# Batch 0 by halves of heads, paired columns and smaller edits at both ends of a fused attention and feed-forward kernel

## The chip, the core and the metric

The kernel runs on one core of a Trainium2 chip. A core has five engines with queues of their own: TensorE (PE in the profile, with its weight loads as PEld), VectorE (DVE), ScalarE (ACT), GpSimd (POOL) and SyncE (SP), which here only issues DMAs. The metric is device time in microseconds for one execution, the median of several runs.

## What is computed

A linear attention (softmax of q over the features of a head, softmax of k over the sequence) feeds a feed-forward layer with a gated activation:

```python
q_s = softmax(q, axis=-1);  k_s = softmax(k, axis=2)          # 8 batches, 8 heads, 576 rows, 64 features
kv  = einsum('bhsd,bhse->bhde', k_s, v)
x   = einsum('bhsd,bhde->bhse', q_s, kv)                      # reshaped to 4608 x 512
h   = x @ w_in                                                # 512 x 2048
g   = h * sigmoid(beta * h)
out = g @ w_out                                               # 2048 x 512, float32
```

Inputs and output are float32; products run in bfloat16 with float32 sums. The sigmoid is made from tanh: g = (tanh(beta h / 2) + 1) h, with a factor two taken out of the attention part.

## The kernel before

**Tiling.** The 4608 rows are nine chunks of 512: the first 512 rows of each of the eight batches, in a layout where a partition holds nine consecutive sequence rows, and one chunk (number 7) that gathers the last 64 rows of all batches. The hidden dimension of 2048 is 16 units of 128. Unit n of the 144 (chunk n // 16, block n % 16) has a first product `h_n` (`st1`, line 867: four matmuls of 512 columns, 128 contraction rows each, weights from `w_in_b`), a tanh on ScalarE (`th_n`, line 899), a gate on VectorE (`g_n`, line 909), and a second product `o_n` (`st2`, line 937: four matmuls, into four PSUM banks `acc` that collect over the 16 units of a chunk). The other four PSUM banks, `ring`, are dealt out in turn (`take`, line 206) to first products, transposes, x blocks and the small products of the attention part.

**Attention per batch.** q: maximum over features (VectorE, line 378), subtraction (GpSimd, 393), exponential (ScalarE, 422), sum (VectorE, 428), reciprocal (433), multiplication (GpSimd, 441), then a transpose: by TensorE for batches 0 and 1 (464), by a DMA from SP for the others (448), which waits until the tail product (`xt`, 734) of the batch two before has read the buffer. k: a maximum by partitions with a 32 by 32 transpose (490), its reduction (`kred`, 501), an exchange between halves of 64 partitions (batch 0: a float32 matmul with a permutation, `kswap`, 507; others: four small reductions, 522), the maximum spread out again (`krep`, 550), subtraction (GpSimd, 560), exponential (612). Then `kv` (638), its scaling (`kvn`, 657 to 660), x (688) and its cast into SBUF (`xev`).

**Batch 0** goes in thirds of the rows (rows 0 to 3, 4 to 7 and 8 of a partition's nine). k of heads 0 to 3 (`KPE`) is subtracted on TensorE: an identity matmul puts k into PSUM (580), a second one with a negative identity adds minus the maximum (593), and the exponential reads PSUM (600, 605). x of batch 0 is made for one half of the rows at a time, all heads; so the first four units (`LEAD`) run by halves of rows: 256 columns, tanh of two units per bank and a gate over two units.

**Weights.** w_in and w_out come in eight blocks w0 to w7 (even: four units of w_in, odd: four units of w_out), each in two DMAs of 512 KB into four buffers `wst`, and are cast to bfloat16 on GpSimd or ScalarE (line 320). A unit's w_in columns are 128 neighbours; its w_out rows too, 2 KB for each.

**Order.** The whole program is one list, `ORDER` (line 17), of named operations, with the engine of some. An engine runs its operations in the order in which they stand there; a DMA stands on SP in the same way. Semaphores hold an operation until its inputs are there, and whatever stands behind it on the same engine waits with it. `fill` operations are matmuls on zeros (or on q's exponentials) whose results nobody reads; they stand before the first unit only.

**End.** In the last chunk the output block t = 3 is made in two halves of 256 columns; the second half sits in a ring bank and is copied in two pieces of 128, each with its own store (`LAST_PIECES`, line 928).

Of the kernel before, what the change touches and what calls it, by code (L numbers as in the profile page):

```python
# [13 lines left out]
EPS = 1e-9  # L14
# [15 lines left out]
qnorm_0_2_1=pool, xev_0_0_1=act, x_0_1_0, fill_10, fill_5, cast_w2_0=pool, ld_w2_1, xev_0_1_0=dve, ld_w1_0, ld_w1_1,  # L30
cast_w2_1=pool, h_0_0_0, h_0_0_1, h_1_0_0, h_1_0_1, h_0_1_0, xev_0_1_1=act, th_0_0, th_1_0, h_0_1_1, qmax_1_2,
h_1_1_0, h_1_1_1, ld_w4_0, g_0_0, ld_w4_1, qmax_1_3, h_2_0_0, h_2_1_0, ld_k1_0, th_0_1, th_1_1, g_0_1, qsub_1_1=pool,
ld_k1_1, h_2_0_1, h_3_0_0, h_3_0_1, th_3_0, th_2_0, g_2_0, h_2_1_1, h_3_1_0, h_3_1_1, th_2_1, h_6, th_3_1, g_2_1,
h_4, qexp_1_1, qsum_1_1, th_4, g_4, h_5, qexp_1_0, th_5, qsum_1_0, h_7, cast_w1_0=pool, ld_w3_0, o_0_1,
cast_w1_1=pool, o_1_1, o_0_0, o_1_0, qexp_1_2, g_5, qtrt_0, o_2_0, qsum_1_2, qrcp_1_0, th_6, th_7, qexp_1_3, g_6,
ld_w6_0, ld_w6_1, o_3_0, o_2_1, o_3_1, cast_w4_0=pool, qnorm_1_0=pool, qtrtev_0_0=act, ld_w3_1, qtrtev_0_1=dve,
qsum_1_3, g_7, qrcp_1_1, qnorm_1_1=pool, cast_w4_1=act, h_8, th_8, cast_w3_0=pool, kmax_1_0, kmax_1_1, g_8,
cast_w6_0=pool, kmax_1_3, kmax_1_2, kred_1, ksmall_1, krep_1, ld_w5_0, qtr_1_0, qtrev_1_0=act, h_10, th_10, h_9,
qtr_1_1, th_9, h_11, g_10, qtrev_1_1=act, o_4, o_5, th_11, ld_w5_1, cast_w6_1=act, ksub_1_0=pool, cast_w3_1=act,
ld_v1_0, ld_v1_1, ld_w7_0, h_14, kexp_1_1, g_11, h_12, h_15, th_14, ld_q2_1, g_9, cast_w5_0=pool, th_12, g_14, g_12,  # L40
h_13, th_13, kexp_1_0, th_15, ksub_1_1=pool, g_15, ld_q2_0, o_6, o_7, o_8, o_9, vcast_1_0=pool, ld_k2_1, g_13,
# [1028 lines left out]
```

## Time and profile before

| | |
|---|---|
| median of 3 runs | 287.04 us (286.77 to 288.16) |
| profiled execution, its own time | 287.31 us |
| its span, first to last instruction | 285.5 us |
| TensorE busy | 275.8 us, 97% |
| VectorE, ScalarE, GpSimd busy | 194.9, 174.2, 131.2 us |
| DMA | 50.01 MB, mean 175 GB/s |
| granted TensorE clock | 0.999 |

The page of the profile has the busy time of each engine, the span in 40 slices of 7.1 us (a digit is a tenth busy), the DMA queues, the chain of work that ended last, and groups of instructions as `line engine operation out<-in shapes xcount | busy us, mean ns of one | idle before, releaser`. In the chain a row is `start us, duration us, what`. In a row by stretches stand the stretch, its length, each engine's busy time with its count (PE, PEld, DVE, ACT, POOL), the granted clock, the share of the DMA engines and GB/s. A row of the timeline is `start us, duration us, engine line operation, count, [idle before, releaser]`; neighbours that overlap are merged in it. A DMA issue has KB and the median time from issue to landing.

### The profile page before, as it was taken

How to read it: one execution, taken by the hardware profiler on the slowest of the kernel's cores; microseconds unless marked ns; L12 is line 12 of the kernel's file. 1: busy time of each engine (PE TensorE's matmuls, PEld its weight loads, DVE VectorE, ACT ScalarE, POOL GpSimd, SP SyncE). 2: the span in 40 equal slices, each digit the busy share in tenths (PEclk: the TensorE clock that was granted, in tenths of full speed). 3: DMA queues.
4: the chain of work that ended last, by engine and by line, in shares of the span. 5: the costliest groups of instructions: out<-in, count | busy, mean ns of one | idle time of the engine just before them, and what ended most of it. 6: DMA issues, size and time to landing. Idle time of an engine off the chain costs nothing.

```text
span 285.5 us, 5163 instructions
## 1 busy us (share of the span) xinstructions
PE 275.8 (97%) x1947; PEld 129.9 (45%) x1977; DVE 194.9 (68%) x394; ACT 174.2 (61%) x291; POOL 131.2 (46%) x93
## 2 busy tenths in 40 slices
PE   7799999999999999999999999999999999999994
PEld 2356544444444544444444544444444444444442
DVE  2998957999899898997667858555754263435421
ACT  2498885887488577837586566564671274345422
POOL 6899996869379948083960650090020000000000
PEclk9999999999999999999999999999999999999999
DMA  7999999990991994991434927000054001005104
GB/s 229 390 391 385 384 389 391 390 336 7 276 371 43 316 275 181 295 329 41 152 119 113 189 62 193 0 3 2 0 141 164 0 0 39 0 0 187 73 0 147
DMA packets 37048, 50.01 MB, mean 175 GB/s; under 512 B 15760, under 2 KB 16160, under 8 KB 37024
## 3 DMA queue, kind: packets, MB, share of 16 engines
q1 hardware_dynamic: 36880, 49.63, 53.4%
q8 instruction: 15, 0.25, 0.3%
q10 hardware_dynamic: 144, 0.07, 0.1%
q14 instruction: 9, 0.07, 0.1%
HBM read 36.71 MB, written 9.44 MB: 162 GB/s over the span
## 4 chain that ended last, share of the span: by engine, by line
PE 91%; DMA 4%; ACT 1%; SPq 1%; issue 1%; DVE 0%
PE hT L889 43%; PE acc L959 42%; DMA kf<-in_k_dram 2%; DMA wst<-in_moe_w_in_dram 2%; PE hT L638 2%; PE hT L688 1%; SPq L275 1%; PE hT L951 1%; PE acc L951 1%; ACT w_in_b L232 0%; PE hT L464 0%; PE hT L734 0%; ACT qT L232 0%; ACT ek L612 0%; ACT ek L605 0%
## 5 line engine op out<-in xcount | busy, mean ns | idle before, releaser
L907 ACT ACTIVATE th<-hT,beta_c 128x512 bf16<-128x512 f32 (+1 forms) x148 | 96.6, 677 | 66.9 <-PE hT L889 48.5
L924 DVE SCALAR_TENSOR_TENSOR g<-th,hT 128x512 bf16<-128x512 bf16 x144 | 94.6, 680 | 58.5 <-ACT th L907 55.5
L959 PE MATMUL acc<-w_out_b,g 128*128 128x512 bf16 x543 | 130.7, 379 | 1.4 <-issue 0.8
L889 PE MATMUL hT<-xT,w_in_b 128*128 128x512 bf16 (+1 forms) x517 | 117.7, 372 | 0.7 <-issue 0.2
L889 PEld LDWEIGHTS <-w_in_b 128*128 128x128 bf16 x592 | 57.6, 98 | 64.8 <-ACT w_in_b L232 0.2
L959 PEld LDWEIGHTS <-g 128*128 128x128 bf16 x560 | 53.7, 98 | 64.5 <-issue 2.9
L560 POOL TENSOR_TENSOR kf<-kf,kmb 128x1152 f32<-128x1152 f32 (+1 forms) x15 | 38.0, 2543 | 23.6 <-DVE kmb L550 17.6
L441 POOL TENSOR_TENSOR qn<-eqe,qz 128x1152 bf16<-128x1152 bf16 (+2 forms) x20 | 34.5, 1739 | 28.0 <-DVE qz L433 18.1
L393 POOL TENSOR_TENSOR qf<-qf,qm 128x1152 f32<-128x1152 f32 (+2 forms) x20 | 34.4, 1733 | 18.4 <-issue 11.9
L378 DVE TENSOR_REDUCE qm<-qf 128x9 f32<-128x576 f32 (+2 forms) x34 | 23.3, 704 | 6.2 <-DMA qf<-in_q_dram 6.2
L422 ACT ACTIVATE eqe<-qf 128x576 bf16<-128x576 f32 (+2 forms) x34 | 21.5, 657 | 9.5 <-POOL qf L393 9.5
L232 ACT CAST xT<-hT 128x512 bf16<-128x512 f32 x19 | 12.6, 740 | 21.1 <-PE hT L688 21.1
L428 DVE TENSOR_REDUCE qs<-eqe 128x9 f32<-128x585 bf16 (+2 forms) x34 | 24.0, 713 | 0.5 <-ACT eqe L422 0.4
L490 DVE TRANSPOSE_TENSOR_REDUCE km<-kf 128x18 f32<-128x576 f32 x32 | 23.6, 754 | 0.0
L612 ACT ACTIVATE ek<-kf 128x576 bf16<-128x576 f32 x30 | 19.5, 683 | 0.9 <-DMA vf<-in_v_dram 0.9
L234 POOL CAST va<-vf 128x1152 bf16<-128x1152 f32 (+1 forms) x11 | 12.0, 1105 | 6.9 <-DMA vf<-in_v_dram 6.9
L889 PE MATMUL hT<-xTt,w_in_b 128*128 128x512 bf16 x63 | 14.9, 379 | 0.1
L234 DVE CAST xT<-hT 128x512 bf16<-128x512 f32 x9 | 6.3, 728 | 7.0 <-PE hT L688 7.0
L232 ACT COPY osb<-acc 128x512 f32<-128x512 f32 x14 | 7.8, 594 | 3.0 <-PE acc L959 3.0
L367 PE MATMUL hT<-g,warm 128*128 128x512 bf16 x21 | 7.0, 482 | 1.6 <-POOL g L240 1.5
L234 DVE COPY osb<-acc 128x512 f32<-128x512 f32 (+1 forms) x6 | 3.8, 632 | 4.9 <-PE acc L951 3.8
L638 PEld LDWEIGHTS <-ek 64*64 64x64 bf16 x576 | 5.7, 106 | 2.2 <-issue 1.3
(74 smaller groups left out, 121.7 us busy)
## 6 DMA issues: line engine op xcount, KB each, us to landing
qf<-in_q_dram SPq DMA_DIRECT2D x14, 576.0 KB, 6.9
kf<-in_k_dram SPq DMA_DIRECT2D x14, 576.0 KB, 7.7
vf<-in_v_dram SPq DMA_DIRECT2D x14, 576.0 KB, 8.4
out_dram<-osb SPq DMA_DIRECT2D x19, 256.0 KB, 2.6
wst<-in_moe_w_in_dram SPq DMA_DIRECT2D x8, 512.0 KB, 7.9
wst<-in_moe_w_out_dram SPq DMA_DIRECT2D x8, 512.0 KB, 11.2
out_dram<-wst SPq DMA_DIRECT2D x16, 256.0 KB, 3.7
qf<-in_q_dram SPq DMA_DIRECT2D x4, 288.0 KB, 4.1
```

Of the source, the lines that this page charges most:

```text
L234: eng.tensor_copy(dst, src)
L378: dve.tensor_reduce(qm[:, j : j + n, i0:i1], qf[b % 2][:, j : j + n, i0:i1], axis=AX.X, op=ALU.max,)
L393: eng.tensor_tensor(x, x, m, ALU.subtract)
L422: act.activation(eq[:, i0:i1, j : j + n, :].rearrange("p i j d -> p j i d"), x, ACTF.Exp)
L428: dve.tensor_reduce(qs[:, i0:i1, j : j + n].unsqueeze(3), x, axis=AX.X, op=ALU.add)
L441: eng.tensor_tensor(qn[b % 2][:, i0:i1, j : j + n, :], eq[:, i0:i1, j : j + n, :], z, ALU.mult)
L490: dve.tensor_reduce(km[:, j : j + n].rearrange("p j i e -> p (j i e)"), kf[b % 2][:, j : j + n].rearrange("p j i (e c) -> p (j i e) c", c=32),
L560: eng.tensor_tensor(x, x, m, ALU.subtract)
L889: pe.matmul(w, w_in_b[:, kt, u * P : (u + 1) * P], r, start=(kt == 0), stop=(kt == KT - 1),)
L907: act.activation(th[turn(n, h) % 3][:, c], bank(n, h), ACTF.Tanh, scale=beta_c[:, u : u + 1])
L924: dve.scalar_tensor_tensor(out=out, in0=of, scalar=1.0, in1=src, op0=ALU.add, op1=ALU.mult)
L959: pe.matmul(acc[t][:], g[n % NG][:, t * P : (t + 1) * P], w_out_b[:, u, :], start=(u == 0), stop=(u == NJ - 1),)
```

## The change

1. **Batch 0 by halves of heads.** `kred`, `kswap`, `ksmall`, `kvn` and x of batch 0 are done for heads 0 to 3 (J = 0) and 4 to 7 (J = 1) apart. x is made for all 512 rows of one half of the features. The TensorE path for k (`KPE`, `k_in`, `k_minus`, `minus`) is gone; k pieces 0 and 2 are subtracted on VectorE, 1 and 3 on GpSimd.
2. **q of batch 0 by bias.** For rows 0 to 3 and 4 to 7 of heads 0 to 3 the maximum is negated and given to the exponential as a bias, one instruction of 64 columns per row and pair of heads (sixteen in all), with no subtraction.
3. **First units by halves of features.** Units 0 to 3 run all 512 columns, with contraction blocks 0 and 1 (heads 0 to 3) apart from 2 and 3. Units 2 and 3 use banks of `acc`. Tanh and gate are those of every other unit.
4. **Batch 1's k by halves**, in the manner of batch 0: two `kswap` matmuls in place of the small reductions, four subtractions of one piece (two on VectorE through PSUM) in place of two of two pieces on GpSimd.
5. **Columns dealt in pairs.** Unit u takes every second column of a 256-column block of w_in (the even or the odd ones) and the w_out rows that match. A partition of w_out then gets two neighbouring rows, 4 KB at a time, and the weight load reads `w_in_b` with a step of two. Each 256-column block in `w_in_b` is followed by 64 unused columns. beta is transposed with the same step.
6. **Last rows in 384 and 128.** Output block t = 3 of the last chunk in two pieces, 384 columns in `acc` and 128 in a ring bank, one copy and one store each.
7. **A new `ORDER`** throughout, with a new order of loads.

```diff
+consts, ld_q0_1, ld_q0_0, qmax_0_0_j1, qmax_0_0_j0, qmax_0_1_j1, qmax_0_2_0, qexp_0_0_j1, ld_q0_3, qexp_0_0_j0,
+ld_q0_2, qsub_0_2_0=pool, qmax_0_1_j0, qsum_0_0_0, qrcp_0_0_0, qexp_0_2_0, qexp_0_1_j1, qexp_0_1_j0, ld_k0_1,
+qmax_0_1_1, qsub_0_1_1=pool, qmax_0_0_1, qsub_0_0_1=pool, ld_beta, ld_k0_0, ld_v0_0, ld_k0_3, ld_v0_1, kmax_0_1,
+kmax_0_0, qsum_0_1_0, ld_k0_2, ld_v0_2, fill_0, fill_5, fill_7, fill_10, fill_14, ld_v0_3, ld_w0_0, kred_0_0,
+qrcp_0_1_0, qexp_0_1_1, fill_12, fill_6, fill_1, qnorm_0_0_0=pool, fill_3, fill_13, fill_4, kswap_0_0, qtr_0_0_0,
+kmax_0_3, ksmall_0_0, krep_0_1, qexp_0_0_1, qsum_0_0_1, qnorm_0_1_0=pool, ld_w0_1, fill_8, qtrev_0_0_0=act, kmax_0_2,
+qtr_0_1_0, vcast_0_j0=act, fill_2, ksub_0_1=pool, qtrev_0_1_0=act, qrcp_0_0_1, krep_0_0, ld_w2_0, ld_w2_1, kred_0_1,
+ld_q1_1, vcast_0_j1=act, kswap_0_1, qnorm_0_0_1=pool, ksub_0_0=dve, kexp_0_1, ksmall_0_1, fill_11, beta_tr, krep_0_3,
+krep_0_2, kexp_0_0, qtr_0_0_1, ksub_0_3=pool, vcast_0_j3=act, cast_w0_0_1=act, qsum_0_1_1, ksub_0_2=dve, kexp_0_2,
+qrcp_0_1_1, kv_0_0, kexp_0_3, kvn_0_0, ld_w1_0, qmax_0_2_1, qtrev_0_0_1=dve, fill_9, x_0_0, xev_0_0=dve,
+vcast_0_j2=pool, kv_0_1, qnorm_0_1_1=pool, cast_w0_1_0=pool, kvn_0_1, qsub_0_2_1=pool, cast_w0_0_0=pool, qtr_0_1_1,
+xev_0_1=act, h_2_0, h_3_0, cast_w2_0=pool, qtrev_0_1_1=act, ld_w1_1, cast_w2_1=pool, x_0_1, xev_0_3=dve, ld_w4_0,
+cast_w0_1_1=act, qexp_0_2_1, qsum_0_2_0, qsum_0_2_1, qrcp_0_2, qnorm_0_2_1=pool, cast_w1_0=pool, h_0_0, h_1_0,
+ld_w4_1, xev_0_2=act, beta_ev, h_1_1, th_1, ld_q1_0, ld_w3_0, h_0_1, qmax_1_2, h_3_1, h_2_1, ld_k1_1, ld_w6_0,
+qmax_1_3, th_0, g_0, th_2, h_5, g_2, th_5, g_1, th_3, ld_w6_1, g_3, qsub_1_1=pool, h_6, h_4, h_7, th_4, g_5, th_6,
+g_4, g_6, ld_w3_1, cast_w1_1=pool, o_0, o_1, o_2, o_3, qnorm_0_2_0=pool, cast_w4_0=pool, qexp_1_2, qexp_1_3,
+qsum_1_3, qsum_1_2, qrcp_1_1, th_7, ld_k1_0, ld_w5_0, qnorm_1_1=pool, ld_w5_1, g_7, cast_w3_0=pool, ld_v1_0,
...
+st_2_2, xt_3, qnorm_6_0=pool, qexp_7_0, qexp_7_1, xtev_3_0=act, kv_5_0, xtev_3_1=dve,
...
+o_142_0, o_137_3_0, o_141_2, o_143_0, o_142_2, o_143_2, o_138_1, o_139_1, oev_8_0=dve, st_7_2, st_8_0, o_138_3_0,
+o_140_1, o_141_1, o_142_1, o_143_1, o_139_3_0, o_140_3_0, oev_8_1=act, o_141_3_0, o_142_3_0, o_143_3_0,
+oev_8_3_0=act, oev_8_2=dve, st_8_2, o_136_3_1, o_137_3_1, o_138_3_1, o_139_3_1, o_140_3_1, o_141_3_1, st_8_1,
+st_8_3_0, o_142_3_1, o_143_3_1, oev_8_3_1=dve, st_8_3_1
...
-    KPE = range(2)
-    QPE = set()
+    BIAS = {(0, 0), (1, 0)}
...
-    w_in_b = sbt("w_in_b", [P, KT, FF], BF16)
+    w_in_b = sbt("w_in_b", [P, KT, NJ // 2, 2 * P + 64], BF16)
...
-    w_out_v = w_out.rearrange("(j p) f -> p j f", p=P)
+    w_out_v = w_out.rearrange("(m p r) f -> p m r f", p=P, r=2)
...
-                for c, (c0, c1) in enumerate(((0, P), (P, 512))):
+                for c, (c0, c1) in enumerate(((0, 2 * P), (2 * P, 512))):
...
+    def q_exp_rows(j, n, i0, i1):
...
+        for a in range(j, j + n):
+            for i in range(i0, i1):
+                act.activation(eq[:, i, a, :], qf[0][:, a, i, :], ACTF.Exp, bias=qm[:, a, i : i + 1])
...
+    def k_swap(b, J):
...
         pe.matmul(
-            place[("swap", b)][:, 0 : 2 * KT],
+            place[("swap", b, J)][:, 0:4],
             swap[:],
-            kmr[:, :, :, 0].rearrange("p j e -> p (j e)"),
+            kmr[:, k_cut(J), :, 0].rearrange("p j e -> p (j e)"),
...
+            for b in range(2):
+                to = pool if j % 2 else dve
+                op(f"krep {b} {j}", lambda b=b, j=j, to=to: k_rep(b, j, 1, to))
+                op(f"ksub {b} {j}", lambda e, b=b, j=j: k_sub(b, j, 1, e), "pool" if j % 2 else "dve")
...
+    def x_mm(b, J):
...
+            for jp in range(2):
+                place[("x", b, 2 * J + jp)] = acc[2 * jp + J][:]
...
+    SPARE = {2: 0, 3: 2}
...
             pe.matmul(
                 w,
-                w_in_b[:, kt, u * P : (u + 1) * P],
-                r,
+                w_in_b[:, kt, u // 2, u % 2 : 2 * P : 2],
+                x[:, kt],
...
-    LAST_PIECES = ((0, 0, 256), (1, 0, 128), (1, 128, 128))
+    PIECES = ((0, 384), (384, 512))
```

More of the change, by code (lines that the diff above doesn't have):

```diff
@@ L382, in q_max @@
             op=ALU.max,
+            negate=minus,
         )
@@ L928 @@
[L928 to L937 removed]
+        v = NJ // 2 * (u % 2) + u // 2
+        uses("st1", n)
+        if n >= 3:
+            uses("gate", n - 3)
+        made("tanh", n)
+        act.activation(th[n % 3][:], place[("h", n)], ACTF.Tanh, scale=beta_c[:, v : v + 1])
```

569 lines of the change are left out of this document (210 added, 359 removed).

## The prediction, made before the changed kernel was run

> **What bounds the kernel now.** I read the page first: the span, the busy shares, and the row of TensorE beside the row of the DMA engines.
>
> ```profile
> span 285.5 us, 5163 instructions
> PE 275.8 (97%) x1947; PEld 129.9 (45%) x1977; DVE 194.9 (68%) x394; ACT 174.2 (61%) x291; POOL 131.2 (46%) x93
> ...
> PE   7799999999999999999999999999999999999994
> ...
> DMA  7999999990991994991434927000054001005104
> ```
>
> The DMA engines are full for eight slices (57 us), yet from the third slice TensorE is full too. So I looked at when the real work begins and what TensorE idles after that: the chain of waits in order of time, then the busy time of each engine by stretches.
>
> ```profile
> 4.03 6.47 DMA kf<-in_k_dram
> ...
> 20.67 7.01 PE hT L889 x48
> ...
> 40.78 4.32 PE acc L959 x20
> ```
>
> ```profile
> 20.67:60.00 39.33, 39.01 (x282) 19.80 (x284) 32.63 (x68) 32.53 (x56) 31.77 (x25) 1.00 1.05 388
> ...
> sum 261.33, PE 259.05 PEld 122.02 DVE 180.65 ACT 162.50 POOL 114.85; mean PE 51.81 PEld 24.40 DVE 36.13 ACT 32.50 POOL 22.97
> ```
>
> The first unit starts at 20.67 us. From there to 282 us TensorE is busy 259.05 of 261.33 us, and one 512-column matmul takes 4.32/20 = 0.216 us. The kernel is thus three terms: a prelude of 20.67 us, in which batch 0 has to come through; some 261 us of TensorE work, which the change does not shorten (the same 1152 matmuls, 248.8 us at 0.216); and a tail. A gain can come from an earlier start and the tail; a loss from TensorE waiting again, or from dearer matmuls.
>
> **When data lands.** One q or k piece of batch 0 is 288 KB. The rows are DMA issues with the time to landing (the first q piece, then the second half of the first weight block), that weight's issue on SP, the first maximum that needs the fourth q piece, and the rate.
>
> ```profile
> qf<-in_q_dram SPq DMA_DIRECT2D x1, 288.0 KB, 2.9
> ...
> wst<-in_moe_w_in_dram SPq DMA_DIRECT2D x1, 512.0 KB, 7.2
> ```
>
> ```profile
> 9.80 1.09 SPq L316 DMA_DIRECT2D wst<-in_moe_w_in_dram  x2
> ...
> 7.63 1.48 DVE L378 TENSOR_REDUCE qm<-qf 128x8 f32<-128x512 f32 x3 [1.68 <-DMA qf<-in_q_dram]
> ...
> 14.00:16.00 2.00, 1.85 (x11) 1.15 (x10) 1.93 (x7) 1.95 (x5) 1.95 (x2) 1.00 1.05 390
> ```
>
> The fourth piece (1.18 MB) lands at about 7.6, the eighth (the chain) at 10.5, and the last of w0, 5.18 MB in all, at about 10.5 + 7.2 = 17.7. All lie near 4.5 + MB/0.39. In the new order q1's first half (0.59 MB) goes behind the weights, so w0's halves land at 14.9 and 16.2 instead of 16.4 and 17.7. The new order of k and v gives k pieces at 8.3, 9.0, 10.5, 12.0 and the last v at 13.5.
>
> **The new prelude, by its queues.** Durations, from the groups kept apart by shape:
>
> ```profile
> L490 DVE TRANSPOSE_TENSOR_REDUCE km<-kf 128x18 f32<-128x576 f32 x32 | 23.6, 754 | 0.0
> L612 ACT ACTIVATE ek<-kf 128x576 bf16<-128x576 f32 x30 | 19.5, 683 | 0.9 <-DMA vf<-in_v_dram 0.9
> L441 POOL TENSOR_TENSOR qn<-eqe,qz 128x512 bf16<-128x512 bf16 x4 | 4.1, 1046 | 0.3
> L393 POOL TENSOR_TENSOR qf<-qf,qm 128x512 f32<-128x512 f32 x4 | 4.1, 1046 | 2.1 <-DVE qm L378 2.1
> L378 DVE TENSOR_REDUCE qm<-qf 128x8 f32<-128x512 f32 x4 | 2.6, 681 | 1.7 <-DMA qf<-in_q_dram 1.7
> L428 DVE TENSOR_REDUCE qs<-eqe 128x8 f32<-128x520 bf16 x4 | 2.6, 674 | 0.0
> L234 DVE CAST xT<-acc 128x512 bf16<-128x512 f32 x2 | 1.4, 740 | 0.2 <-ACT beta_c L349 0.2
> L560 POOL TENSOR_TENSOR kf<-kf,kmb 128x576 f32<-128x576 f32 x1 | 1.4, 1411 | 0.1
> L560 DVE TENSOR_TENSOR kf<-kf,hT 128x576 f32<-128x576 f32 x1 | 0.7, 715 | 0.0
> L378 DVE TENSOR_REDUCE qm<-qf 128x2 f32<-128x128 f32 x2 | 0.6, 284 | 4.5 <-DMA qf<-in_q_dram 4.5
> L422 ACT ACTIVATE eqe<-qf 128x128 bf16<-128x128 f32 x2 | 0.5, 302 | 1.7 <-POOL qf L393 1.7
> L501 DVE TENSOR_REDUCE kmr<-km 128x8 f32<-128x72 f32 x8 | 1.8, 224 | 0.1
> L550 DVE STREAM_TRANSPOSE hT<-kmx 128x64 f32<-128x64 f32 x1 | 0.3, 260 | 0.0
> L530 DVE TENSOR_TENSOR kmx<-kmr,hT 128x8 f32<-128x8 f32 x1 | 0.2, 151 | 0.0
> ```
>
> VectorE is the tightest queue. From the fourth q piece at 7.6 it runs, without a gap, two maxima of q, four of k, three sums, two subtractions of k (now one piece each), and eleven small operations (four spreads at 0.26, the rest 0.15 to 0.22): 1.36 + 3.02 + 2.02 + 1.43 + 2.29 = 10.1 us by means. Neighbours overlap by about 0.07 (a 1.48 us row for what are 0.68 + 0.68 + 0.28 by means), 22 of them 1.5 us, so it ends near 16.2. GpSimd runs beside it (two q subtractions, four q divisions, two k subtractions, one v cast, the fourth division ending near 18.0). ScalarE ends the last exponential of k at about 17.7.
>
> Heads 0 to 3 are through first: their k-by-v product is done at about 15.9, its scaling on VectorE 16.1 to 17.0, their two x blocks are in SBUF at 18.5 (0.74 each, one on VectorE, one on ScalarE). Units 2 and 3 then run two of their four matmuls each, 0.86 us from 18.6. The second half's scaling ends at 19.1, its x product at 19.7, its casts at 20.6. Meanwhile units 0 and 1 run two matmuls each (weights cast at 19.6). From 20.7 TensorE has all it needs, with 8 matmuls (1.73 us) behind it: as good as a start at 18.97. **Term 1: 18.97 − 20.67 = −1.7 us**, bounds −2.3 and −0.9 (one k exponential sooner; or 0.1 us more at each of eight hand-overs between engines).
>
> The sixteen exponentials with a bias replace two 512-wide ones and two GpSimd subtractions. No row shows 64 columns; the 128-wide row gives 0.30 as an upper bound. Sixteen at that are 4.8 us, begun at 4.2 (the first q piece lands at 0.7 + 2.9, its maximum takes under 0.68) and over by 9.0 at worst, ahead of the sum that needs them (10.2). Cover: the wait for k. They cost nothing; the identity-matmul path removed for k (L580, L593) freed TensorE only where it was waiting.
>
> **Batch 1's k by halves.** Two more small matmuls land in the full stretch, in float32 with four columns. Batch 0 has one; its two passes, its two loads and the matmul behind it:
>
> ```profile
> 13.42 0.39 PE L507 MATMUL hT<-kmr,swap 128*128 128x8 f32 x2
> 13.66 0.59 PE L367 MATMUL hT<-eqe,warm 128*128 128x512 bf16 x2
> ```
>
> ```profile
> 13.42 0.30 PEld L507 LDWEIGHTS hT<-kmr,swap 128*128 128x128 f32 x2
> ```
>
> It holds TensorE for 13.66 − 13.42 = 0.24 us; bounds 0 and 0.39. **Term 2: 2 × 0.24 = +0.5 us.** The two subtractions that move to VectorE (0.715 each) lie beside GpSimd's two of 1.41 and in a stretch where VectorE is 32.63 of 39.33 us busy; nothing on the path, unless that slack is gone (a rival).
>
> **The first stage of units** needs weights in the old sequence 1.7 us sooner. Counting 0.863 us per unit from 18.97, the first output matmul falls at 25.9: its tanh and gate of unit 3 are through at about 25.5, w1's first cast at 23.0. Unit 13 falls at 35.2, w6 is cast by GpSimd at about 34.8; output 6 at 37.8, w3's second half cast at about 37.2. All in time, by 0.4 to 0.6 us; I take 0, bounds 0 and +1.
>
> **Transposes by DMA.** Batch 5's must wait until batch 3's tail product has freed its buffer; then x of batch 5 needs it.
>
> ```profile
> 157.64 0.18 PE hT L734 x8
> ...
> 165.57 0.56 PE hT L688 x8
> ```
>
> ```profile
> 157.93 4.02 SPq L448 DMA_TRANSPOSE qT<-qn  x1
> ...
> DMA to landing us min/median/max: 4.5/5.5/8.4
> ```
>
> Now there are 165.57 − 157.64 = 7.9 us for it, of which output 70 is 0.86; the new order puts output 70 ahead, leaving 7.1. At 5.5 to 8.4 plus 0.3 of issue the wait is 0 to 1.6. **Term 3: +0.2 us**, nearer the median.
>
> **Strided weights.** Every first-stage weight load now reads every second column. No bf16 load with a step stands in the trace; the bounds are:
>
> ```profile
> L889 PEld LDWEIGHTS <-w_in_b 128*128 128x128 bf16 x592 | 57.6, 98 | 64.8 <-ACT w_in_b L232 0.2
> L580 PEld LDWEIGHTS acc<-kf,ident_f 128*128 128x128 f32 x4 | 0.7, 188 | 1.3 <-issue 1.2
> ```
>
> 98 ns contiguous; 188 for float32, which reaches over the same 512 bytes of a partition. Both lie under the 216 ns of the matmul that runs meanwhile. And the two float32 loads above, 188 each, took 0.30 together, so they follow at about 0.11. I take 0; cover gone, 90 ns on 576 loads would be 52 us, a bound that the overlap excludes. [...]
>
> w_out's 4 KB rows in place of 2 KB: the rate is 390 GB/s with either input now, so 0.
>
> **Tail.** The last bank was copied in two pieces, one after the other:
>
> ```profile
> 281.92 0.28 ACT osb L232
> 282.21 0.29 DVE osb L234
> ```
>
> Now one copy of 128 columns follows the last matmul: **term 4: −0.3 us**, bounds 0 (the 192 KB store just ahead lands last) and −0.3.
>
> **Sum.** −1.7 + 0.5 + 0.2 − 0.3 = −1.3 us on the profiled execution's 287.31 (285.5 span and 1.8 around it): 286.0. It stands 0.27 above the median 287.04, so against that 285.7.
>
> **Rivals.** (a) *Nothing is given back*: the small matmuls hide behind loads, the transpose keeps its cover, the start reaches its early bound: −2.3 − 0.3 = −2.6, 284.4. For it: VectorE's list is the only tight one; against: the 0.24 is measured. (b) *The start is eaten*: margins of 0.4 to 0.6 us at output 0, unit 13 and output 6 are less than the hand-over error of the working; if each is overrun by 0.5, +1.5, so +0.2: 287.2. (c) *GpSimd becomes the bound from 27 to 38 us*, the slower one. Its queue holds a q division of batch 1 (2.1 us) that waits for VectorE's sums, ahead of the casts of w3 and w6. It decides once that wait exceeds 0.5 us; from there each microsecond is one of TensorE. With two more VectorE subtractions and eleven small steps of k in that stretch, 4 us late gives −1.3 + 3.5 = +2.2: 289.2. For it: GpSimd is busy 31.77 of 39.33 us there. Against: before, batch 1's divisions waited 0.6 us only:
>
> ```profile
> 29.66 4.31 POOL L441 TENSOR_TENSOR qn<-eqe,qz 128x1152 bf16<-128x1152 bf16 x2 [0.58 <-ACT th L907]
> ```
>
> (d) *Strided loads outlast their cover*: from 216 ns on; at 226, 10 ns × 576 = +5.8, 291.5. Against: both bound rows.
>
> **How the numbers follow.** Half a per cent, 1.4 us, is about what can be told from no change: faster is below 285.6, slower above 288.5. Forecast 0.45 (own range 284.9 to 286.6; 0.25 below 285.6, since two bounds of term 1 and the transpose's median lie on the low side), (a) 0.20, (b) 0.12, (c) 0.16, (d) 0.07. Faster 0.25 + 0.20 = 0.45; same 0.20 + 0.12 = 0.32; slower 0.23. The range runs from 284.2, just below (a), to 289.2 at (c), and leaves out (d) and the worst of (c).
>
> **What would show it.** Term 1: the first pair of unit matmuls near 18.6 us and an unbroken run from 20.7; wrong if VectorE has gaps after 7.6 or the run starts past 21.5. Term 2: two L507-like matmuls costing 0.2 to 0.4 us each. Term 3: TensorE idle ahead of x of batch 5. Strided loads: the mean of the w_in_b load, and 0.216 us per matmul in the stretch after 220 us; at 0.22 or more (d) holds. (b) and (c): TensorE idle in 20 to 60 us above the 0.3 of before, with a release by GpSimd or VectorE. Tail: one copy and at most 3.3 us between last matmul and end.

## The result, and the profile after

| | before | after |
|---|---|---|
| median | 287.06 us (286.77 to 288.16) | 290.50 us (290.16 to 290.79) |
| profiled execution, its span | 287.31, 285.5 us | 290.16, 288.1 us |
| granted clock, whole span | 0.999 | 0.988 |
| TensorE, VectorE, GpSimd busy | 275.8, 194.9, 131.2 us | 278.9, 201.4, 124.7 us |
| first output matmul starts | 27.52 us | 28.05 us |
| batch 1's k-by-v product starts | 45.03 us | 47.05 us |
| last matmul ends | 281.88 us | 284.51 us |

The ratio is 1.0112 with a 95% interval of 1.0089 to 1.0136: slower by 1.1%, where 0.5% faster was forecast. The lower rows of the table place the loss in the two profiled executions: the first output is 0.5 us late instead of 1.7 us early, the next stretch, up to batch 1's k-by-v product, takes 19.00 us instead of 17.51 (1.5 more), what follows takes 0.6 more, and the tail is unchanged. That is 2.6 us of the 3.44 between the medians: the profiled execution of before lies above its median, and that of the changed kernel is its shortest. The two starts in TensorE's timeline of the kernel before:

```profile
27.52 1.89 PE L959 MATMUL acc<-w_out_b,g 128*128 128x512 bf16 x7
...
45.03 0.78 PE L638 MATMUL hT<-va,ek 64*64 64x65 bf16 x72
```

The page of the changed kernel, with its busy shares, TensorE by slices of 7.2 us, and the granted clock by slices in tenths:

```profile
span 288.1 us, 5152 instructions
PE 278.9 (97%) x1950; PEld 127.5 (44%) x1950; DVE 201.4 (70%) x413; ACT 175.4 (61%) x297; POOL 124.7 (43%) x88
...
PE   7789989999999999999999999999999999999995
...
PEclk9969999999999999999999999999999999999999
```

TensorE's slices look as good as before. The row to read is PEclk: a 6 in the third slice. TensorE was busy there, at a lower clock. The kernel before has no such slice:

```profile
PEclk9999999999999999999999999999999999999999
```

The same place by stretches of the changed kernel (stretch, length, busy time and count of PE, PEld, DVE, ACT, POOL, granted clock, DMA share, GB/s):

```profile
10.00:15.00 5.00, 3.53 (x49) 2.00 (x52) 4.93 (x17) 4.17 (x8) 5.00 (x5) 1.00 1.04 377
15.00:16.00 1.00, 0.64 (x33) 0.24 (x21) 0.93 (x7) 1.00 (x3) 1.00 (x2) 0.93 1.06 401
16.00:17.00 1.00, 0.77 (x6) 0.38 (x6) 0.73 (x5) 1.00 (x3) 1.00 (x2) 0.50 1.05 389
...
22.00:23.00 1.00, 1.00 (x4) 0.39 (x3) 0.97 (x5) 0.01 (x1) 0.92 (x2) 0.65 1.03 375
23.00:24.00 1.00, 1.00 (x7) 0.44 (x5) 0.96 (x2) 0.43 (x1) 1.00 (x2) 1.00 1.02 367
```

From 15.9 us (0.93 in that microsecond) to 22.7 us (0.65) the clock is half: 6.8 us. In the kernel before it stays at 1.00 up to 280 us. The timeline of TensorE in the changed kernel, first units, first outputs, unit 13 and batch 1's product:

```profile
18.74 1.89 PE L789 MATMUL acc<-xT,w_in_b 128*128 128x512 bf16 x4 [0.49 <-POOL w_in_b L230]
20.56 0.64 PE L624 MATMUL acc<-qT,kvn 64*64 64x512 bf16 x4
21.13 2.77 PE L789 MATMUL hT<-xT,w_in_b 128*128 128x512 bf16 x8
...
28.05 3.62 PE L853 MATMUL acc<-w_out_b,g 128*128 128x512 bf16 x16
...
37.13 0.28 PE L494 MATMUL hT<-kmr,swap 128*128 128x4 f32 x2
38.35 3.00 PE L789 MATMUL hT<-xT,w_in_b 128*128 128x512 bf16 x12 [0.94 <-POOL w_in_b L230]
...
43.78 0.28 PE L494 MATMUL hT<-kmr,swap 128*128 128x4 f32 x2
43.92 2.75 PE L853 MATMUL acc<-w_out_b,g 128*128 128x512 bf16 x12
...
47.05 0.78 PE L579 MATMUL hT<-va,ek 64*64 64x65 bf16 x72
```

The first unit matmuls come at 18.74, close to the 18.6 that was forecast. But four of them take 1.89 us instead of 0.86, and the eight at 21.13 take 2.77 instead of 1.73. On GpSimd (first row) and on TensorE's weight loads (second) stand two waits that belong to nothing the units need:

```profile
20.69 2.02 POOL L230 CAST w_in_b<-wst 128x1024 bf16<-128x1024 f32 x2 [2.01 <-PE acc L789]
```

```profile
21.79 0.13 PEld L789 LDWEIGHTS <-w_in_b 128*128 128x128 bf16 x2 [0.55 <-POOL w_in_b L230]
```

The casts of w2 (units 4 to 7) wait 2.01 us for matmuls of units 2 and 3, which read w0; then a load of w0's columns waits 0.55 us for a cast of w2. They share a tile, `w_in_b`, and no byte.

### The profile page after: what moved, and what is told of

It is laid out like the page before. It is cut to its first block, busy times and chain, and to the rows that moved or that the text cites. A ratio compares the mean times of both kernels' runs of the same rounds, so it can differ in the third digit from the quotient of the medians.

```text
span 288.1 us, 5152 instructions
## 1 busy us (share of the span) xinstructions
PE 278.9 (97%) x1950; PEld 127.5 (44%) x1950; DVE 201.4 (70%) x413; ACT 175.4 (61%) x297; POOL 124.7 (43%) x88
## 4 chain that ended last, share of the span: by engine, by line
PE 88%; POOL 4%; DVE 3%; ACT 1%; DMA 1%; issue 1%; DVEq 0%; POOLq 0%
PE hT L789 41%; PE acc L853 41%; PE hT L579 2%; PE hT L624 1%; POOL qn L422 1%; POOL w_in_b L230 1%; DVE g L814 1%; DMA qf<-in_q_dram 1%; PE acc L789 1%; PE acc L845 1%; POOL qf L385 1%; DVE qm L369 1%; POOL kf L548 1%; DVE qs L409 1%; ACT eqe L403 1%
## 5 line engine op out<-in xcount | busy, mean ns | idle before, releaser
L806 ACT ACTIVATE th<-hT,beta_c 128x512 bf16<-128x512 f32 x142 | 93.9, 689 | 68.8 <-PE hT L789 43.1
L853 PE MATMUL acc<-w_out_b,g 128*128 128x512 bf16 x560 | 134.2, 380 | 0.0
L789 PE MATMUL hT<-xT,w_in_b 128*128 128x512 bf16 x504 | 119.0, 381 | 1.1 <-POOL w_in_b L230 0.9
L385 POOL TENSOR_TENSOR qf<-qf,qm 128x1152 f32<-128x1152 f32 (+2 forms) x18 | 32.3, 1807 | 7.2 <-DVE qm L369 4.1
L369 DVE TENSOR_REDUCE qm<-qf 128x9 f32<-128x576 f32 (+3 forms) x36 | 23.4, 671 | 3.9 <-DMA qf<-in_q_dram 3.9
L555 ACT ACTIVATE ek<-kf 128x576 bf16<-128x576 f32 x32 | 21.3, 684 | 0.1
L230 POOL CAST va<-vf 128x1152 bf16<-128x1152 f32 (+1 forms) x8 | 8.7, 1084 | 18.5 <-DMA vf<-in_v_dram 17.5
L228 ACT CAST va<-vf 128x1152 bf16<-128x1152 f32 (+1 forms) x10 | 10.2, 1018 | 0.1
L228 ACT COPY osb<-acc 128x512 f32<-128x512 f32 (+1 forms) x11 | 6.0, 588 | 6.5 <-PE acc L853 6.3
L230 DVE COPY osb<-acc 128x512 f32<-128x512 f32 x9 | 6.0, 686 | 3.2 <-PE acc L853 3.1
```

What stands on the lines that cost most here:

```text
L228: act.copy(dst, src)
L230: eng.tensor_copy(dst, src)
L369: dve.tensor_reduce(qm[:, j : j + n, i0:i1], qf[b % 2][:, j : j + n, i0:i1], axis=AX.X, op=ALU.max, negate=minus,)
L385: eng.tensor_tensor(x, x, m, ALU.subtract)
L789: pe.matmul(w, w_in_b[:, kt, u // 2, u % 2 : 2 * P : 2], x[:, kt], start=(kt == 0), stop=(kt == KT - 1),)
L806: act.activation(th[n % 3][:], place[("h", n)], ACTF.Tanh, scale=beta_c[:, v : v + 1])
```

## The experiments

Times are medians; "before" ran beside every kernel at 287.05 to 287.38 us. Where the weight tile is split, a line has a number one higher than in the changed kernel.

**1. Zero matmuls, tiles, queues: one repair at a time.** The theory was three causes: the clock, the shared tile, and weight casts queued behind q and k work at unit 13.

```diff
# e1_fills: ten more zero matmuls in the prelude
-fill_8 1, fill_9 1, fill_11 1, fill_2 2
+fill_8 3, fill_9 3, fill_11 2, fill_2 4, fill_15 1 (behind beta_tr), fill_16 2 (behind qtr_0_1_1)
# e2_tiles: five weight tiles in place of one
-w_in_b = sbt("w_in_b", [P, KT, NJ // 2, 2 * P + 64], BF16)
+w_in_t = [sbt(f"w_in_b{i}", [P, KT, 1 if i < 2 else 2, 2 * P + 64], BF16) for i in range(5)]
# e3_queue
-qsub_1_0=pool, ... cast_w6_0=pool, ... qexp_1_0, cast_w6_1=act
+cast_w6_0=pool, qsub_1_0=pool, ... cast_w6_1=act, qexp_1_0
# e4_all: all three;  e6_fills_tiles: the first two
```

> The changed kernel with nine more zero matmuls (nobody reads them) in the gaps of TensorE between 11 and 18.7 us. Theory A (clock): in the changed kernel the granted clock was 0.50 from about 15.8 to 22.7 us, because TensorE had too little to do before; full clock makes the first four unit matmuls 0.86 us in place of 1.90 and the rest of that stretch about 0.9 shorter, so 290.5 - 2.0 = 288.5, with the clock at 1.0 from 15 to 23 us. Rival B (queue): the first units wait for GpSimd's casts (18.7 and 21.7 us) whatever the clock, so under 0.7 us is gained: 289.8 or more. If the clock stays at 0.50 the matmuls were too few and nothing is told.

> The changed kernel with the w_in weights in five tiles (two of one 256-column block, three of two) in place of one; same sizes, same order. Theory D (shared tile): units 2 and 3 waited 0.49 us for the cast of the block of units 0 and 1, that cast's follower waited 2.01 us for the matmuls of units 2 and 3, and units 0 and 1 then waited for it until 21.8, though none of them touches the same bytes. Apart, the first unit starts near 18.2, GpSimd's gap of 2.0 us at 18.7 is gone, and 0.5 to 1.0 us is gained: 289.5 to 290.0, the clock still at 0.50 there. Rival: the waits are for the bytes themselves, and the time stays at 290.5.

> The changed kernel with two entries of the order moved: GpSimd casts w6 ahead of the q subtraction of batch 1 heads 0 to 3, and ScalarE casts its half of w6 ahead of that q's first exponential. Theory C (GpSimd bound, rival c of the prediction): unit 13 waited 0.94 us for the first cast and again for the second (TensorE busy 4.00 of 5.00 us from 35 to 40); both waits go and 1.0 us is gained: 289.5. Rival: the subtraction, now 1 us later, delays batch 1's transposes and k by v product by as much, and nothing is gained: 290.5.

> All three edits together. If the clock (2.0), the shared tile (0.5 to 1.0) and the queue (1.0) are the loss and add up, 290.5 - 3.7 = 286.8, level with the kernel before (287.0) or just under it. If they overlap, because GpSimd's queue sets the next thing anyway, 288 to 289.

> The changed kernel with the nine more zero matmuls and with w_in in five tiles, without the reordering of GpSimd's and ScalarE's queues. Theory (clock and false waits explain the start, the queue edit alone shifted the loss from the weight casts to the ring of banks): the start as with all three edits (first output matmul near 25.7 us), and 287.9 to 288.6 us, at most 0.6 above the run with all three. Rival (the queue edit is worth its 1 to 2 us once the start is right, since only then does unit 13 come early enough to wait for its weights): 289 us or more, with a wait of TensorE for a cast of 1 us or more ahead of unit 13.

| kernel | median us | ratio to before, interval | clock, profiled | first output | k-by-v product of batch 1 |
|---|---|---|---|---|---|
| changed | 290.50 | 1.0112 [1.0089, 1.0136] | 0.988 | 28.05 | 47.05 |
| e1_fills | 289.46 | 1.0086 [1.0065, 1.0108] | 1.000 | 27.42 | 46.42 |
| e2_tiles | 288.56 | 1.0048 [1.0033, 1.0063] | 0.993 | 26.35 | 45.35 |
| e3_queue | 290.65 | 1.0126 [1.0106, 1.0145] | 0.982 | 28.27 | 47.37 |
| e4_all | 287.95 | 1.0034 [1.0018, 1.0051] | 1.000 | 25.69 | 44.86 |
| e6_fills_tiles | 287.77 | 1.0029 [1.0017, 1.0040] | 1.000 | 25.52 | 44.53 |

The edit adds ten zero matmuls (the expectation says nine). They are worth 1.04 us with one tile (290.50 to 289.46) and 0.79 with five (288.56 to 287.77); the five tiles 1.94 and 1.69. The first expectation was twice too high, the second twice too low. The two causes sit in the same 5 us and are not apart: with the five tiles alone the clock was already 0.993 in place of 0.988. Together they return 2.73 of the 3.44 us lost, and the start is then as forecast. TensorE's timeline in the kernel with both:

```profile
18.15 1.03 PE L790 MATMUL acc<-xT,w_in_b 128*128 128x512 bf16 x4
19.11 0.41 PE L625 MATMUL acc<-qT,kvn 64*64 64x512 bf16 x4
19.45 1.92 PE L790 MATMUL hT<-xT,w_in_b 128*128 128x512 bf16 x8
...
25.52 3.62 PE L854 MATMUL acc<-w_out_b,g 128*128 128x512 bf16 x16
...
35.83 3.00 PE L790 MATMUL hT<-xT,w_in_b 128*128 128x512 bf16 x12 [0.94 <-POOL w_in_b L230]
...
44.53 0.78 PE L580 MATMUL hT<-va,ek 64*64 64x65 bf16 x72
```

The first output is 2.0 us ahead of the kernel before (27.52); the product at 44.53 only 0.5. The queue edit gained nothing, alone or beside the others: with all three edits the wait for a cast gives way to waits for VectorE.

```profile
35.57 2.81 PE L790 MATMUL hT<-xT,w_in_b 128*128 128x512 bf16 x12 [0.52 <-DVE g L815]
...
41.49 0.39 PE L495 MATMUL hT<-kmr,swap 128*128 128x4 f32 x2 [0.33 <-DVE kmr L489]
```

**2. The paired columns by themselves**, put into the kernel before. Were they free, as forecast, and where do the false waits come from: the step of two, or the padding and its four-dimensional tile?

```diff
# e5_pairs_alone: before + pairs, padding, 4 KB rows, first cast of w0 256 wide
-w_in_b[:, kt, u * P : (u + 1) * P]
+w_in_b[:, kt, u // 2, u % 2 : 2 * P : 2]
# e9_step_nopad: the step without the padding (tile and casts as before)
+w_in_b[:, kt, 2 * P * (u // 2) + u % 2 : 2 * P * (u // 2 + 1) : 2]
# e12_pad_nostep: the padding without the step
+w_in_b[:, kt, u // 2, P * (u % 2) : P * (u % 2) + P]
# e10_pairs_tiles: e5 with the five tiles
```

> The kernel before with one part of the change alone: paired feature columns (first-stage weight loads with a step of two, 64 columns of padding, the biases to match, second-stage weights in 4 KB rows, w0's first cast 256 columns wide instead of 128). Theory (the loss lies in the new prelude and in two queues, the strided loads are free): 286.9 to 287.4 us, mean of the first-stage weight load 98 ns, 0.216 us per matmul. Rival (strided loads cost something that adds up over 576 of them, 2 ns each or more): 288.2 us or more, with the mean load above 100 ns.

> The kernel before with the paired columns, the 4 KB rows and the 256-column first cast as in the run of the pairs alone, but the weight tile without the 64 columns of padding: tile and casts as in the kernel before, only the reads step by two. Theory (the false waits come from how the padded, four-dimensional tile is tracked, not from the step): 287.0 to 287.6 us, no wait of a cast for units that read other columns, mean weight load 98 to 99 ns. Rival (a read with a step is tracked as a wider range and makes the false waits by itself): 294 us or more, with TensorE waiting over 5 us for casts of w_in.

> The kernel before with the padded tile and its four-dimensional cast alone: columns not paired, reads contiguous, rows of 2 KB. Theory (the padding makes the false waits): 294 us or more, the same waits for casts as with the pairs alone. Rival (the step makes them): 287.0 to 287.6 us.

> The kernel before with the pairs, the padding and the 4 KB rows as in the run of the pairs alone, and w_in in five tiles, so that no cast can be ordered behind another block's reads. Theory (all 9 us of the pairs alone are false waits and the clock that falls with them; the loads and the rows themselves are free): 286.9 to 287.6 us, the same as before within 0.2%. Rival (part of the 9 us belongs to the strided loads or to the 4 KB rows): 288.2 us or more at a clock of 0.998 or above.

| kernel | median us | ratio to before, interval |
|---|---|---|
| e5_pairs_alone | 296.26 | 1.0320 [1.0301, 1.0339] |
| e9_step_nopad | 296.74 | 1.0338 [1.0313, 1.0363] |
| e12_pad_nostep | 287.21 | 0.9999 [0.9985, 1.0012] |
| e10_pairs_tiles | 287.36 | 1.0000 [0.9985, 1.0016] |

The rival was right: the step alone costs over 9 us in the order of before, and the padding nothing. What TensorE waited for with the pairs alone (engine, line, released by: us in total, times, longest), then the longest of these waits and the cast that ends it:

```profile
PE hT L893 <- POOL w_in_b L234: 5.5, 3, 3.2
```

```profile
39.34 3.17 PE L893 MATMUL hT<-xT,w_in_b 128*128 128x512 bf16 x7 [3.21 <-POOL w_in_b L234]
```

```profile
38.24 1.04 POOL L234 CAST w_in_b<-wst 128x1024 bf16<-128x1024 f32 x1
```

A unit of w4 starts when the cast of w6 ends (38.24 + 1.04 = 39.28), because that cast stands ahead of it in the order. In the step without padding the same line reads 5.6, 3, 3.2. The waits are 5.5 of the 9 us. The rest fits the clock: in the profiled execution with the pairs alone the granted clock was 0.71, 0.95, 0.96 and 0.87 from 20 to 25, 25 to 30, 30 to 40 and 40 to 50 us. By estimate from these it halves twice for 3.4 us, from 22.1 and from 39.2 us, at the two longer waits (1.7 and 3.2 us), and 2 × 1.7 us are lost. With five tiles the waits all but go (0.3 us is left), and the clock was 0.998 or more in all twelve executions. So a read with a step is taken by the program as a read of more than it touches, and is ordered against casts of other blocks, in both directions. With five tiles the whole price is gone, and so the loads themselves are free. Their row there (weight loads, count, busy, mean ns of one):

```profile
L894 PEld LDWEIGHTS <-w_in_b 128*128 128x128 bf16 x592 | 57.5, 98 | 65.5 <-POOL w_in_b L234 0.8 <-ACT w_in_b L232 0.2 <-issue 0.2
```

**3. The clock, in the kernel before.** Does the fall belong to the new prelude, or does any prelude that leaves TensorE idler get it?

```diff
# e8_before_thin: eleven of the sixteen later zero matmuls out;  e15_before_nofill: all sixteen (the edit shown)
-FILLS = [(14, None)] + [(2, (h, J)) ...] + 8 * [(1, None)]
+FILLS = [(14, None)] + [(0, (h, J)) ...] + 8 * [(0, None)]
```

> The kernel before with nine of its sixteen later zero matmuls left out (they compute nothing that is used), all other work and its order kept. Theory (the clock falls when TensorE is busy two thirds or less over some 6 us, whoever's kernel it is; in the kernel before, the zero matmuls and the float32 identity matmuls of k kept it up): granted clock 0.5 for some us between 13 and 24 us, the first unit's matmuls at 0.45 us each while it lasts, and 288 to 290 us. Rival (the fall belongs to the new prelude's order alone): clock 1.00 throughout and 287.0 to 287.3.

> The kernel before without any of its sixteen later zero matmuls (they compute nothing that is used); only the first fourteen stay. Theory (the clock follows how busy TensorE was in the last few us, so that without them it falls in nearly every run): clock 0.985 to 0.995 in every run, granted clock 0.50 in a stretch between 13 and 23 us, 288.3 to 290 us. Rival (the clock of the kernel before does not depend on them): 0.998 or more and 287.0 to 287.5 us.

| kernel | median us | executions with a clock under 0.995 | TensorE busy from 8 to 18 us, profiled execution |
|---|---|---|---|
| e11_repaired (section 4) | 288.08 | none of 10 | 9.67 us |
| e6_fills_tiles | 287.77 | none of 9 | 9.09 us |
| e4_all | 287.95 | 2 of 10 | 8.66 us |
| e7_vector (section 4) | 288.60 | 2 of 7 | 8.27 us |
| e1_fills | 289.46 | 1 of 4 | 8.10 us |
| before | 287.16 | none of 96 | 8.06 us |
| changed | 290.50 | 4 of 4 | 7.43 us, part of it at half clock |
| e2_tiles | 288.56 | 4 of 4 | 7.43 us, part of it at half clock |
| e15_before_nofill | 287.12 (ratio 1.0005 [0.9992, 1.0019]) | 9 of 10 | 6.96 us |
| e8_before_thin | 287.81 (ratio 1.0025 [1.0009, 1.0041]) | 6 of 12 | 6.68 us |

Both expectations were half right (the thinned kernel leaves out eleven zero matmuls, not nine). The clock does fall in the kernel before once TensorE is less busy, but not in every execution; the profiled one of each was at 1.00. The ten added zero matmuls make a fall rarer, not impossible: of the kernels that have them, e1, e4 and e7 fell in 5 of 21 executions, e6 in none of 9. In the thinned kernel the six executions with a fall have a median of 288.40 us, the other six 287.41: it costs 1.0 us there. And without any of the sixteen zero matmuls the fall costs nothing on balance: the first output then starts at 26.85 instead of 27.52 where the clock holds, since some zero matmuls stand on the path, and the lower clock takes about that back. A clock of 0.994 over 286 us is 0.006 × 286 = 1.7 us lost, by estimate half rate for 3.4 us; the changed kernel's 0.988 is twice that, 6.9 us, and its stretches show 6.8. In e2 (0.993) the granted clock was 0.65, 0.50, 0.50 and 0.65 in the four microseconds from 16 to 20 us, which is 3.4 us at half rate. What sets these lengths, and why a kernel falls in some executions and not in others, no run shows.

**4. The stretch from the first output to batch 1's product.** Four orders, a late start, and less VectorE work:

```diff
# e7_vector: e4_all + VectorE relieved from 32 to 41 us
-g_9, g_8, kmax_1_2, h_10, h_11, kmax_1_3, kred_1_1, th_11, g_11, th_10, g_10, ... o_5, kswap_1_1, ... h_13
+g_9, g_8, h_10, h_11, th_10, g_10, kmax_1_2, th_11, g_11, kmax_1_3, kred_1_1, ... o_5, h_13, kswap_1_1
-qtrev_1_1=dve, qsum_1_0, ... g_12, kmax_1_0
+qtrev_1_1=act, kmax_1_0, qsum_1_0, ... g_12
# e11_repaired: e7 + cast_w3_1 ahead of ksub_1_3, four more zero matmuls
# e13_late_start: e11 + seven zero matmuls right ahead of the first unit
# e14_less_vector: e11 without two q and two k maxima of batch 1
+if b == 1 and j < 2: return          (q_max);   if b == 1 and j in (0, 2): return   (k_max)
# e16_order: e11 with krep_1_2 and ksub_1_2 ahead of the q sums, cast_w5 earlier, kswap_1_0 behind o_8, o_11 ahead of kv_1
```

> As the run with all three edits, and VectorE relieved from 32 to 41 us: the gates of units 10 and 11 go ahead of the last k maxima, unit 13 ahead of the first swap of batch 1, one q copy goes to ScalarE, and one k maximum moves into VectorE's wait for the q exponential. Theory (after the repair, what is left is VectorE: 0.5 us at unit 13 and 0.5 us at the second swap): both waits of TensorE go, batch 1's k-by-v product starts near 44.0 instead of 44.9, and the time is 286.8 to 287.3, no slower than the kernel before. Rival (VectorE, ScalarE and GpSimd together are full in this stretch, the wait moves to the exponentials of k or to the cast of w6): 287.7 to 288.3, with a new wait of 0.5 us or more between 34 and 46 us.

> The run with the relieved VectorE, its cast of w3's second half put ahead of the k subtraction on GpSimd, and four more zero matmuls in the prelude's gaps. Theory (the 1.25 us at output 6 was that cast's place in the queue; the scatter of that run was the clock): no wait above 0.4 us between 20 and 50 us, batch 1's k-by-v product near 43.9 us, 286.4 to 287.0 us and a clock of 0.998 or more in all runs, so a little faster than the kernel before. Rival (the three engines are full here, and the k chain then comes late): the product at 44.7 us or later with TensorE waiting for an exponential of k or the swap, 287.3 to 288.0 us.

> The last repaired kernel with seven more zero matmuls right ahead of the first unit (they compute nothing that is used), so that the units start 1.5 us later, at about 19.8. Theory (batch 1's steps, not the start, set when its k-by-v product can run; the start's lead is lost there whatever happens): that product still near 45.0 us and the whole kernel within 0.4 us of the repaired one, 287.9 to 288.5. Rival (the lead is worth its time and the stretch's waits are its own): 1.2 to 1.5 us more, 289.2 to 289.7.

> The last repaired kernel without two of the q maxima and two of the k maxima of batch 1 (older maxima are subtracted in their place, so batch 1's output is not the reference's): 2.8 us less of VectorE between 30 and 41 us, nothing else changed. Theory (VectorE is the bound of this stretch): batch 1's k-by-v product by 44.2 us instead of 45.0, and 286.8 to 287.4 us. Rival (the transfers pace the stretch: the DMA engines are full, w6 and k of batch 1 land just in time, so a lighter VectorE waits for them): the product at 44.7 us or later and 287.7 us or more.

> The last repaired kernel (all work in it) with one more order between 36 and 45 us: the k subtraction that holds a bank goes ahead of the q sums on VectorE, which wait for ScalarE's q exponentials, w5's two casts go earlier on ScalarE and GpSimd, the second swap goes behind output 8, and output 11 ahead of batch 1's k-by-v product. Theory (what holds TensorE in this stretch is the order of the queues around four banks, not the throughput of any one engine): the 1.1 us wait ahead of unit 14 goes, output 11 starts near 43.5 us, and 286.8 to 287.3 us. Rival (the stretch is full: v of batch 1 lands at about 41.5 and its casts, q division and k subtraction then come one after the other on busy engines): the product starts at 45 us or later after output 11 with a wait of 0.5 us or more, and 287.6 to 288.3 us.

| kernel | median us | ratio to before, interval | first output to product | longest wait of TensorE in it, for |
|---|---|---|---|---|
| before | 287.16 | | 17.51 us | none |
| changed | 290.50 | 1.0112 [1.0089, 1.0136] | 19.00 | 0.94, cast of w6 |
| e6_fills_tiles | 287.77 | 1.0029 [1.0017, 1.0040] | 19.01 | 0.94, cast of w6 |
| e7_vector | 288.60 | 1.0075 [1.0042, 1.0109] | 19.11 | 1.25, cast of w3 |
| e11_repaired | 288.08 | 1.0042 [1.0026, 1.0057] | 19.38 | 1.10, k subtraction |
| e13_late_start | 289.24 | 1.0076 [1.0060, 1.0091] | 19.06 | 0.85, k subtraction |
| e14_less_vector | 287.61 | 1.0018 [1.0006, 1.0030] | 19.12 | 0.72, k subtraction |
| e16_order | 288.67 | 1.0050 [1.0036, 1.0063] | 19.17 less output 11 | 0.94, gate |

Each order removed the wait that it aimed at and met another of the same size. One row of TensorE's timeline from each of e7, e11 and e16, and from e16 the row of GpSimd behind it:

```profile
39.07 1.02 PE L854 MATMUL acc<-w_out_b,g 128*128 128x512 bf16 x4 [1.25 <-POOL w_out_b L230]
```

```profile
39.67 1.02 PE L790 MATMUL hT<-xT,w_in_b 128*128 128x512 bf16 x4 [1.10 <-DVE kf L549]
```

```profile
44.44 0.61 PE L444 MATMUL hT<-ident,qn 128*128 128x128 bf16 x8 [0.94 <-DVE g L815]
```

```profile
39.66 1.04 POOL L230 CAST w_out_b<-wst 128x1024 bf16<-128x1024 f32 x1 [1.25 <-DMA wst<-in_moe_w_out_dram]
```

The late start overturned the idea that the lead is worthless: starting 1.5 us later cost 1.16 us, and the stretch became only 0.3 us shorter. The changed kernel, e1, e2 and e6 say the same: they have one order in this stretch and their first outputs lie between 25.52 and 28.05 us, yet it takes 19.00 or 19.01 us in all four. So its end isn't pinned to a moment, as it would be if transfers alone paced it. Taking 2.8 us from VectorE gave 0.47 us, so VectorE's amount of work isn't the whole bound either. e7's times spread from 287.9 to 291.7 us, and its two longest executions had a clock of 0.992 and 0.988; with the further zero matmuls of e11 the clock stayed at 0.998 or more. No repaired kernel is faster than the one before.

## Why the prediction was wrong, point by point

**Term 1, the start (−1.7 us): sized right, but it had two preconditions that failed.** With the false waits and the clock repaired, the first output starts 2.0 us early, inside the bounds of 0.9 to 2.3. In the changed kernel as it stands it starts 0.5 late.

**"Strided weights … I take 0": the first step that failed.** The loads were priced, and rightly: the changed kernel's row reads 98 ns, as before, so rival (d) is out.

```profile
L789 PEld LDWEIGHTS <-w_in_b 128*128 128x128 bf16 x576 | 56.0, 98 | 69.5 <-POOL w_in_b L230 2.3 <-issue 1.7 <-ACT w_in_b L228 0.6
```

The order that the program derives from the stepped reads was not. It is the largest single cause: 1.7 to 1.9 us here, and in the old order, which places casts of later blocks ahead of units of earlier ones, 5.5 us of waits and 3.4 us of the clock. The idle column of this row holds 2.3 us for casts on GpSimd, where the row of before names none; 1.0 of it is unit 13's wait for its own weights and is still there with five tiles, the other 1.3 is not.

**"The identity-matmul path removed for k freed TensorE only where it was waiting": the second.** True of the time, but the term had no place for the clock. The path was 4.9 us of TensorE's work between 9.1 and 16.8 us. Without it TensorE was busy 4.68 us from 9.0 to 15.86 us, where the kernel before has 5.48, and the clock halved at 15.9, 2.8 us ahead of the first unit. That is worth 0.8 to 1.0 us, less than the 3.4 us lost by the clock itself, since part of it fell on a TensorE that was waiting anyway. That the added zero matmuls raise the clock again is shown: with one tile a fall in 4 of 4 executions becomes 1 of 4, with five tiles 4 of 4 becomes none of 9. That the removed path brought the fall on is argued: e8 and e15 keep the path, leave out zero matmuls, and fall too.

**"The first stage of units … I take 0", bounds 0 and +1: the third.** With term 2 it is 1.5 us. With the start repaired (e6) unit 13 could have run at 34.9 us, close to the 35.2 of the forecast, but GpSimd's cast of w6 ended at 35.8 and not at 34.8, and TensorE idled 0.94. Rival (b) had this place and size (+1.5), and (c) its most visible mechanism, GpSimd's q division waiting for VectorE ahead of the casts of w3 and w6:

```profile
32.13 2.13 POOL L422 TENSOR_TENSOR qn<-eqe,qz 128x1152 bf16<-128x1152 bf16 x1 [3.24 <-DVE qz L414]
```

Rival (c)'s 0.58 us of before has become 3.24. By its price, one microsecond of TensorE for each above 0.5, that would be 2.7 us; TensorE idled 0.94, and moving the casts of w6 ahead of a q subtraction and an exponential (e3, e4) returned nothing. What fed it was costed at nothing: the first half of batch 1's q goes behind the weights, so its maxima, exponentials and sums, and two k subtractions taken from GpSimd, all fall into this stretch. VectorE's load there (third busy time) before and after, from the row by stretches of each kernel:

```profile
27.52:45.10 17.58, 17.48 (x101) 8.41 (x105) 13.18 (x28) 15.59 (x24) 16.24 (x12) 1.00 1.05 387
```

```profile
28.05:47.12 19.07, 18.07 (x105) 8.79 (x107) 18.01 (x36) 15.43 (x24) 14.84 (x11) 1.00 1.04 395
```

VectorE has 13.18 of 17.58 us before, 18.01 of 19.07 after. TensorE (first busy time) idles 0.10 us before and 1.00 after; its other 0.6 us is busy time, the swaps among it. The forecast counted spare time of VectorE from the row of before and moved work into it without adding up. What exactly sets the length of 19.0 to 19.4 us stays open: not one queue's order (four were tried), not VectorE's work alone, not the arrival of data alone.

**Term 2, the two swaps (+0.5): at most about 0.4.** The second holds TensorE from 43.78 to 43.92, 0.14 us. The first stands just ahead of a wait in the changed kernel; in another order (e11), without that wait, it takes 0.23, as in batch 0.

**Term 3, the transpose of batch 5 (+0.2): 0.** TensorE does not wait there.

**Bias exponentials (0): right.** Eight in 2.03 us of the chain, 0.25 each, ahead of what needs them:

```profile
4.09 2.03 ACT eqe L403 x8
```

**Term 4, the tail (−0.3): 0.** From the last matmul's end to the span's end it is 3.59 us after, 3.62 before. One copy of 0.29 is saved, as forecast:

```profile
283.89 0.61 PE L845 MATMUL hT<-w_out_b,g 128*128 128x128 bf16 x8
...
284.53 0.29 DVE L230 COPY osb<-hT 128x128 f32<-128x128 f32 x1 [1.86 <-PE hT L845]
284.86 0.66 ACTq L887 DMA_DIRECT2D out_dram<-osb  x1
```

But the store behind it goes through ScalarE's queue (0.66 us to issue) and lands in 2.2 us, where the two last stores of before, one on each queue, took 2.0. The gain of 0 is a bound that was given, though for another reason (the 192 KB store landing last); neither reading is tested.

**The last 0.6 us**, from batch 1's product to the last matmul (236.85 before, 237.46 after, 237.45 in e6), were not forecast. In e6 they and the 1.5 us of the stretch use up the 2.0 us of the start: its span is 285.5 us, that of before. Two tail transposes of batch 0 that used to run ahead of this point now run behind it (0.2 to 0.3 us); the rest isn't located.

## What to carry to other kernels

Before changing how a tile is read, ask what the program's ordering will make of the new range, not only what the access costs: a step of two over a shared tile cost nothing per load (98 ns with it and without) and 9 us in false waits and the falls of the clock that came with them, and five tiles in place of one removed it. Work that "runs while TensorE waits" may be what holds its clock (here TensorE was busy 4.68 of 6.86 us instead of 5.48, and the clock fell to 0.50), so look at the busy share of the few microseconds ahead of the full stretch before taking such work out. And when a prelude is shortened by moving loads back, add up what each engine now has to do in the stretch after it, for a lead of 2.0 us there was down to 0.5 twenty microseconds later.

## What the runs showed of the hardware

The clock fell to half without a long pause: from 9 us to the fall at 15.9 us no idle time of TensorE in the changed kernel's timeline is above 0.5 us, and from 10 to 15 us it was still busy 3.53 of 5 us. It came back only at 22.7 us, though TensorE had been nearly full since 18.7 (busy 3.91 of 4.00 us). And the busy time of those microseconds does not settle the clock: in the kernel before, five zero matmuls left gave a fall in half of the executions and none left in nine of ten, though TensorE was busy 6.68 us of the ten from 8 us in the first and 6.96 in the second; and with 8.1 to 8.7 us e1, e4 and e7 fell in 5 of 21, while before with 8.06 fell in none of 96.
